# An attention-like kernel on one core: loads of batches 1 to 4 issued first on GpSimd, weight casts moved into the schedule, PSUM banks reserved, the DMA queue modelled

## The chip, the cores and the metric

The kernel runs on one core of a Trainium2 chip. The metric is the device time of one execution in microseconds (us), median of several; the span that the profiler shows is some 2 us shorter. Fast executions of one kernel agree within about 0.5 % of each other on the first chip, so a version is compared with runs of the kernel before that were made on the same chip in the same rounds. A few executions fall in a slow state (over 1.5 % above the fastest of the same kernel, as 169.73 us beside 165.76 for before) and are left out of ratios.

## The reference, cut to what matters

Eight batches of 4224 rows of 192 channels. Each row is first mixed with the six rows before it (one softmax over 7 taps for each of 8 heads); then comes linear attention without a softmax, and an output product.

```python
# x: (8, 4224, 192), weight: (8, 7), w_q and w_k: (192, 64), w_out: (192, 192)
w   = softmax(weight)                                # per head, over the 7 taps
y   = sum_k w[h, k] * x_pad[:, s + k, h, :]          # causal, 6 zero rows in front
wq, wk = y @ w_q, y @ w_k
W   = (1 / 8) * wq @ wk.T                            # no softmax on it
out = relu(W @ y) @ w_out
```

Since nothing nonlinear stands between the two products, `W @ y` is computed as `wq @ (wk.T @ y)`, and `wk.T @ y = w_k.T @ (y.T @ y)`. The kernel's names follow: `Y` (the 7-tap mix, as banded matmuls from `xw`), `G` = y.T y, `GS`/`GT` (G copied to SBUF, and transposed parts of it), `M` = the small matrix from G and w_k, `Q` = y w_q, `Z` = relu(Q M), `O` = Z w_out.

## The kernel before

All instructions are put in order at build time by a list scheduler. It keeps a clock for each engine and, at every step, places the job whose inputs it believes ready first. What it believes of data from DMA is a table of constants. Each engine's stream is thus fixed, and in the traces an instruction that waits holds what stands behind it: in experiment 8 ScalarE stands 1.50 us for w_k, and the copies of Y that come after its casts begin only at 17.17 us.

```python
CLOCK = {   # when the schedule believes that things are there, us
    "x0": (6.0, 7.4, 7.9, 9.0, 10.2, 12.3, 14.2, 15.5), "band": 6.5, "wq": 7.0, "wk": 17.0,
    "wo": 20.0, "x": (20.6, 10.3), "store": 5.0, "now": 0.05, "hold": 1.5, "fill": 24.0,
    "issue": 3.2,
}
# ... batch 0 is loaded in eight pieces x0_0 to x0_7, every later batch in two halves
ident = pool(lambda e: e.memset(IDENT[:, :], 0.0))
ident = pool(lambda e: e.affine_select(IDENT[:, :], ...), [ident])
z_zr  = pool(lambda e: e.memset(ZR[:, :, 1, :], 0.0))
zero = {1: clear(1)}                  # two memsets on GpSimd
load(1, 0)                            # first half of batch 1: DMAs issued by GpSimd
# ... jobs are defined ...
cast("wk", WK[:, 0], twice(WST[:, 0, 0:DH]), [wl[1]])     # six casts of w_k on GpSimd
# ...
load(1, 1)                            # second half of batch 1
cast("wo", WO1[:, :], WST[:, 2, :], [wl[2]])              # four casts of w_out on GpSimd
# ...
for b in range(2, 1 + AHEAD):         # AHEAD = 2
    for part in range(2):
        prefetch(b, part)             # clear and load batch 2
# later batches: two batches ahead, after the job that duplicates Y of a half batch
if kind == "D" and job.name[1] > 0:
    prefetch(job.name[1] + AHEAD, job.name[2])
```

GpSimd thus does three things: it issues all loads of x, it casts the weights to bf16, and it makes the duplicates of Y (`COPY y<-y`). The stores are issued by SyncE.

## Time and profile before

| kernel before | |
|---|---|
| time, median of 3 runs | 166.16 us (165.76 to 169.73) |
| span of the profiled run, granted clock of TensorE | 164.8 us, 0.943 |
| TensorE busy | 144.3 us, 88 % |
| real matmul work (see below) | 131.9 us |
| start of the first matmul with data / of the last matmul | 6.6 / 157.1 us |

The page's own summary: TensorE busiest, and half of the chain that ended last is TensorE. "PE" is TensorE, DVE VectorE, ACT ScalarE, POOL GpSimd; the shares of the second line are of the span.

```profile
span 164.8 us, 5806 instructions
...
PE 144.3 (88%) x2518; PEld 108.4 (66%) x2547; DVE 114.7 (70%) x218; ACT 127.4 (77%) x224; POOL 68.5 (42%) x99
...
PE 50%; ACT 23%; DMA 8%; POOL 6%; issue 5%; DVE 3%; ACTq 0%; POOLq 0%
```

Busy time hides how much of it is useful: the page counts a `G` matmul as busy for 193 ns on average, and where nothing holds them they follow each other every 29 ns. So I use a second measure in this text, **work done**: the weight loads of the trace in program order, each matmul taken at the pitch at which its kind recurs where nothing holds it (a 512-column one 0.219 us, a 432-column one 0.184, a 384-column output 0.168, a `G` 0.029, a `Q` 0.0186); the rows of `warm` matmuls (the expectations say "warming"), whose results nothing reads, count nothing. The whole kernel is 131.9 us of work. "Lost" is the time on the clock less the work done by then.

The DMA view of 0 to 45 us, in 40 slices of 1.1 us, shows the hole that the change is aimed at: the rate falls to 148, 130, then 127 and 38, then 19 and 88 GB/s.

```profile
DMA  0059999999999999996999938999999999999999
GB/s 0 10 94 141 198 181 188 188 188 187 189 205 148 130 196 209 194 127 38 184 189 194 175 19 88 193 190 193 189 155 303 349 263 184 334 351 238 193 198 190
```

GpSimd's timeline says why (columns: start, us taken, engine, line, operation, out<-in, count, and in brackets the idle time before with what ended it). It waits 2.15 us for w_k and casts for 2.15 us before it issues batch 1's second half at 18.59, and comes to batch 2 at 23.82.

```profile
16.50 2.15 POOL L797 CAST wk<-wst 128x128 bf16<-128x128 f32 x6 [2.15 <-DMA wst<-in_moe_w_k_dram]
18.59 1.78 POOL L265 DMA_DIRECT2D xw<-in_x_dram  x2
...
23.82 4.78 POOL L265 DMA_DIRECT2D xw<-in_x_dram  x6 [0.30 <-POOL xw L442]
28.58 0.69 POOL L281 DMA_DIRECT2D xw<-in_x_dram  x1
```

The chain of waits of 36 to 56 us (start, us, what) shows where this load lateness reaches TensorE: the last piece of batch 2, issued at 28.58, lands at 42.20, and TensorE's timeline has it waiting for that for 1.19 us before 42.34. ("Issue" is time in which an engine waits for nothing that the profile shows.)

```profile
28.58 13.62 DMA xw<-in_x_dram
42.20 0.14 issue
```

```profile
16.10 0.45 PE L595 MATMUL ps<-yb,wq 32*64 32x288 bf16 x15 [0.69 <-issue]
...
42.34 0.32 PE L530 MATMUL ps<-xw,band 128*128 128x384 bf16 x1 [1.19 <-DMA xw<-in_x_dram]
44.79 0.36 PE L743 MATMUL ps<-wo,zt 128*128 128x192 bf16 x2 [1.17 <-ACT y L898]
```

Note for later what is *not* there: between 15 and 42 us no wait of TensorE is put down to a load of x in this timeline. (Sooner than 15 us batch 0's pieces are waited for, much of it under `warm` matmuls; the change leaves those loads alone.)

### The profile page before, as it was taken

The numbers are of one execution on the slowest core, as the hardware profiler recorded it, in microseconds if no ns is written. First come the engines' busy times: TensorE is split into PE (matmuls) and PEld (weight loads), VectorE is DVE, ScalarE is ACT, GpSimd is POOL, SyncE is SP. The second block draws the span as 40 slices with busy tenths as digits, with TensorE's granted clock in tenths as the row PEclk, the third lists the DMA queues.
The fourth block names the chain that finished last, engine by engine and source line by source line (L and its number), as shares of the span: only waits on it lengthen the run. The fifth ranks groups of instructions, "written<-read, shape, count | busy, mean of one in ns | idle before, by whom it ended". The sixth has DMA issues, their size and how long they took to land.

```text
span 164.8 us, 5806 instructions
## 1 busy us (share of the span) xinstructions
PE 144.3 (88%) x2518; PEld 108.4 (66%) x2547; DVE 114.7 (70%) x218; ACT 127.4 (77%) x224; POOL 68.5 (42%) x99
## 2 busy tenths in 40 slices
PE   5897879699499998999899998999999989999920
PEld 4886734477377777677577866777777767766710
DVE  6784849769467677789788876877967686585500
ACT  5552559686589898788888997979998968799940
POOL 7984989888871807063804562202011200000000
PEclk9999999999999999999999999999999999999996
DMA  3999999999999999999999999999985472678896
GB/s 48 190 188 167 166 162 112 190 275 285 193 191 285 260 225 290 337 231 296 243 330 265 309 223 344 296 282 204 358 309 187 191 279 107 219 296 338 311 397 237
DMA packets 48281, 40.44 MB, mean 245 GB/s; under 512 B 38144, under 2 KB 40320, under 8 KB 48256
## 3 DMA queue, kind: packets, MB, share of 16 engines
q0 software_dynamic: 36784, 13.63, 70.2%
q1 hardware_dynamic: 11472, 26.45, 44.2%
q8 instruction: 20, 0.33, 0.7%
q14 instruction: 5, 0.04, 0.1%
HBM read 27.73 MB, written 25.95 MB: 326 GB/s over the span
## 4 chain that ended last, share of the span: by engine, by line
PE 50%; ACT 23%; DMA 8%; POOL 6%; issue 5%; DVE 3%; ACTq 0%; POOLq 0%
PE ps L624 12%; ACT o_sb L898 8%; DMA xw<-in_x_dram 8%; PE ps L530 8%; PE ps L595 7%; PE ps L743 7%; ACT y L898 7%; PE ps L745 6%; PE ps L700 5%; ACT zt L901 4%; POOL xw L265 4%; PE ps L499 2%; DVE y L898 2%; ACT zr L901 1%; DVE shift L405 1%
## 5 line engine op out<-in xcount | busy, mean ns | idle before, releaser
L898 ACT CAST y<-ps 128x864 bf16<-128x864 f32 (+5 forms) x59 | 48.2, 832 | 6.2 <-PE ps L499 3.1
L898 ACT COPY o_sb<-ps 128x768 f32<-128x768 f32 (+1 forms) x54 | 41.1, 783 | 6.2 <-PE ps L745 5.5
L743 PE MATMUL ps<-wo,zt 128*128 128x192 bf16 x256 | 43.1, 251 | 3.1 <-ACT y L898 1.3
L902 DVE TENSOR_SCALAR zt<-ps 128x512 bf16<-128x512 f32 x52 | 34.4, 684 | 13.4 <-PE ps L700 9.1
L745 PE MATMUL ps<-wo,zt 128*128 128x384 bf16 x128 | 42.5, 332 | 0.0
L265 POOL DMA_DIRECT2D xw<-in_x_dram x51 | 40.7, 803 | 2.1 <-POOL xw L442 1.3
L898 POOL COPY y<-y 128x1152 bf16<-128x1152 bf16 x14 | 16.1, 1148 | 57.6 <-ACT y L898 41.0
L624 PEld LDWEIGHTS ps<-y 128*128 128x128 bf16 x864 | 33.2, 98 | 9.9 <-issue 1.4
L624 PE MATMUL ps<-y 128*128 128x64 bf16 x864 | 36.7, 193 | 0.6 <-DVE y L898 0.2
L743 PEld LDWEIGHTS ps<-wo,zt 128*128 128x128 bf16 x256 | 25.5, 115 | 12.7 <-ACT o_sb L898 1.4
L896 DVE STREAM_TRANSPOSE yb<-y 128x576 int32<-128x576 int32 x48 | 33.7, 748 | 0.2 <-ACT y L898 0.2
L530 PE MATMUL ps<-xw,band 128*128 128x432 bf16 (+1 forms) x112 | 29.3, 340 | 2.0 <-DMA xw<-in_x_dram 1.2
L901 ACT ACTIVATE zt<-ps 128x512 bf16<-128x512 f32 x44 | 26.2, 622 | 0.9 <-PE ps L700 0.8
L700 PE MATMUL ps<-qt,m_sb 128*128 128x512 bf16 x67 | 22.7, 390 | 2.9 <-ACT y L898 0.9
L898 ACT CAST qt<-ps 128x576 bf16<-128x576 f32 (+2 forms) x23 | 12.2, 565 | 12.4 <-PE ps L595 12.3
L898 DVE CAST qt<-ps 128x234 bf16<-128x234 f32 (+1 forms) x25 | 9.6, 423 | 12.3 <-PE ps L595 12.2
L898 DVE COPY o_sb<-ps 128x768 f32<-128x768 f32 (+1 forms) x18 | 14.8, 821 | 4.7 <-PE ps L745 3.4
L595 PE MATMUL ps<-yb,wq 32*64 32x288 bf16 x768 | 16.0, 287 | 1.9 <-issue 1.5
L898 DVE CAST y<-ps 128x864 bf16<-128x864 f32 (+3 forms) x13 | 11.6, 896 | 5.1 <-PE ps L530 3.5
L745 PEld LDWEIGHTS ps<-wo,zt 128*128 128x128 bf16 x128 | 14.5, 113 | 0.0
L530 PEld LDWEIGHTS ps<-xw,band 128*128 128x128 bf16 x112 | 9.8, 99 | 6.6 <-DVE yb L896 1.3
L595 PEld LDWEIGHTS ps<-yb,wq 32*64 32x64 bf16 x768 | 10.5, 103 | 4.5 <-issue 2.4
(74 smaller groups left out, 113.3 us busy)
## 6 DMA issues: line engine op xcount, KB each, us to landing
out_dram<-o_sb SPq DMA_DIRECT2D x31, 768.0 KB, 7.2
xw<-in_x_dram POOLq DMA_DIRECT2D x21, 384.0 KB, 15.3
xw<-in_x_dram POOLq DMA_DIRECT2D x7, 432.0 KB, 17.3
xw<-in_x_dram POOLq DMA_DIRECT2D x4, 240.0 KB, 5.1
out_dram<-o_sb SPq DMA_DIRECT2D x16, 48.0 KB, 5.7
out_dram<-o_sb SPq DMA_DIRECT2D x2, 384.0 KB, 3.5
xw<-in_x_dram POOLq DMA_DIRECT2D x8, 42.0 KB, 9.4
xw<-in_x_dram POOLq DMA_DIRECT2D x1, 288.0 KB, 5.4
```

The source lines that it names most:

```text
L265: return e.dma_start(XW[lo:hi, b % NX, half, c : c + n, :], bass.AP(x_t, at, [[D, hi - lo], [CW * D, n], [1, D]]),)
L499: last = e.matmul(o, band_[:, h, :], rhs, start=True, stop=True, skip_group_check=True)
L530: last = e.matmul(o.rearrange("p (c h d) -> p h c d", h=2, d=GRP), band_[:, h, :], rhs, start=True, stop=True, skip_group_check=True,)
L595: last = e.matmul(PS[64 * h : 64 * h + 64, bk + i, 0:288], WQ[r, j, :], rhs, start=j == 0, stop=j == 5, skip_group_check=True)
L624: last = e.matmul(PS[:, 7, 64 * k : 64 * k + 64], y[:, 64 * k : 64 * k + 128], y[:, 64 * k : 64 * k + 64], start=c + h + k == 0, stop=c == ...
L700: return e.matmul(PS[:, bk, :], m[:, parts[k] : parts[k] + 128], q, start=True, stop=True)
L743: e.matmul(o[:, 192 * h : 192 * h + 192], z[:, h, cols], WO1[:, :], start=h == 0, stop=False, **kw)
L745: last = e.matmul(o[:, 0:384], z[:, 2, cols], WO2[:, :], start=False, stop=True, **kw)
L896: return e.transpose(o, i)
L898: return e.copy(o, i) if eng == "act" else e.tensor_copy(o, i)
L901: return e.activation(o, i, AF.Relu)
L902: return e.tensor_scalar(o, i, 0.0, None, op0=ALU.max)
```

## The change

The intent: keep the load queue full. GpSimd issues the loads of batches 1 to 4 first, one after the other; the casts of w_k and w_out become jobs of the schedule, which gives them to ScalarE or VectorE; the zero rows of batches 1 and 2 are cleared by ScalarE; w_k and w_out are loaded a little earlier. The schedule gets a model of the DMA queue (a rate, a delay, loads and stores sharing it) in place of fixed times for x. The stream of `Q` jobs is asked first at each step, so that its four banks are reserved before another job takes them, and some cost constants are new.

```diff
 CLOCK = {
-    "x0": (6.0, 7.4, 7.9, 9.0, 10.2, 12.3, 14.2, 15.5), "band": 6.5, "wq": 7.0, "wk": 17.0,
-    "wo": 20.0, "x": (20.6, 10.3), "store": 5.0, ...
+    "x0": (6.0, 7.7, 8.2, 9.4, 10.6, 12.5, 13.5, 14.3), "band": 6.6, "wq": 7.1, "wk": 14.0,
+    "wo": 17.0, ...
+    "dma": (377e3, 13.8, 1.6, 0.8),
 }
...
-        wload(2 * s, 0, 128, src, 0, wd, wl[s + 1], [xg[0][3 + 2 * s]])
+        wload(2 * s, 0, 128, src, 0, wd, wl[s + 1], [xg[0][2 + 2 * s]])
...
-    zero = {1: clear(1)}
     load(1, 0)
+    load(1, 1)
+    ident = pool(lambda e: e.memset(IDENT[:, :], 0.0))
+    ...                                       # affine_select, z_zr
+    for b in range(2, NX):                    # NX = 5
+        load(b, 0)
+        load(b, 1)
...
-    cast("wk", WK[:, 0], twice(WST[:, 0, 0:DH]), [wl[1]])
-    ...
-    load(1, 1)
-    cast("wo", WO1[:, :], WST[:, 2, :], [wl[2]])
-    ...
+    casts = [
+        job_w("wk", 0, WK[:, 0], twice(WST[:, 0, 0:DH]), 128, 1),
+        ...
+    ]
...
     streams = {
+        "Q": [job_q(b, g) for b in range(B) for g in range(2)],      # was behind "Z"
+        "W": casts,
...
-    EASY = {"act": 1.0, "dve": 0.3, "pool": 2.0}
+    EASY = {"dve": 0.55, "pool": 1.3}
...
+    RATE, at0, DELAY, LAND = CLOCK["dma"]
+    def flow():                               # shares RATE between loads and stores
+        ...
-                if key[1] > 0:
+                if key[1] > 1:                # duplicates of batch 1 no longer on GpSimd
                     eng = "pool"
...
-            prefetch(job.name[1] + AHEAD, job.name[2])
+            prefetch(job.name[1] + NX - 1, job.name[2])
```

The diff moves far fewer lines than instructions: since the schedule decides by its clocks, the whole order changes. In the order as built TensorE does batch 1's Y and half of batch 2's before the first output matmul.

## The prediction

> **What bounds the kernel now.** From about 55 us on, TensorE: the chain of waits there is mostly matmuls, and Q products recur every 17.2 us per batch (71.9, 89.0, 106.8, 124.2, 140.6 us). Summing matmul columns at the pitch of the timeline (512 columns in 0.224 us, a Q group in 0.89) gives 132 us of real work, 16.6 per batch. It runs between 6.6 and 157.5 us; the last evacuation and store take the other 7.3 us of the 164.8 us span. So TensorE loses about 19 us, mostly early: by 55.5 us it has done 35 us of work, 13.6 lost since 6.6; later it loses 5.
>
> **Why the early stage loses.** The load queue starves because GpSimd issues late. While loads are queued the DMA rate is about 188 GB/s of bf16 written (376 read), but the 0 to 45 us window shows 130 at 14 us, 38 near 18.5, 19 and 88 near 26 to 28. The GpSimd timeline has the causes: memsets and the affine select (9.2 to 11.3), a 2.15 us wait for w_k and 2.15 us of casts (14.4 to 18.6) ahead of batch 1's second half, wo casts and clears up to 23.8 ahead of batch 2. That is some 3.6 us of idle queue. Batch 2's second half then meets the first stores and lands at 42.3, 13.6 us after its last issue, with TensorE waiting. [...] from 34 to 42 us loads and stores together read and write an estimated 375 GB/s.
>
> **What the change does.** GpSimd issues batches 1 to 4 nearly back to back (5.5 us each), from 9.2 to about 32 us, so the queue should not starve. A half batch takes 4.5 to 4.7 us at 376 GB/s: batch 1 lands near 19.5 and 24, batch 2 near 28.5 and 33. The ten casts (0.3 us each) and batch 1's copies go to ScalarE and VectorE: some 5 us more on two engines, between 14 and 33 us, where I estimate both nearly full. In the built order TensorE does batch 1's Y, most of its G, half its Q and half of batch 2's Y before the first output matmul (now at 27.2 us); stores start later. Work, tail order and the 6.6 us start are unchanged.
>
> **Sum.** At 33.5 us I expect 21 us of work done, against 18; the wait at 42 and gaps around it go, so 35 us is reached near 48.5 instead of 55.5. From these 7 us I give back 2 for waits on ScalarE and VectorE and for full overlap of loads and stores (52 MB at 375 GB/s is 139 us). Net 5 us.
>
> **Predicted:** 161 us, range 158 to 164.5; faster by over 2%: 0.76; within 2%: 0.21; slower: 0.03.
>
> **What would show it.** Right: DMA full from 3 to 45 us; no TensorE wait on x after 30 us; batch 2's second Q group 5 to 7 us earlier; 17.2 us per batch later; the same tail. Wrong: TensorE waiting for batch 2's x while output matmuls that could fill the gap stand behind it; ScalarE and VectorE saturated; output copies waiting for stores.
>
> **What would make it wrong.** Landings later than the schedule's model, met by an in-order TensorE[...].

7 us won less 2 given back is net 5, from about 166 us to 161. The 375 GB/s is the author's estimate; the trace of before has, from 34 to 42 us, 0.73 MB of loads (bf16 as written; the f32 read is twice that) and 1.53 MB of stores, together 374 GB/s. The 52 MB are x read and the result written, 25.95 MB each.

## The result, and the profile after

| | before | after |
|---|---|---|
| time, median | 166.16 us (165.76 to 169.73, 4 runs) | 163.89 us (163.59 to 164.41, 4 runs) |
| ratio of fast runs, 95 % interval | | 0.9874 (0.9837 to 0.9912) |
| span of the profiled run, granted clock | 164.8 us, 0.943 | 162.4 us, 0.977 |
| first output matmul | 27.2 us | 38.5 us |
| batch 2's second `Q` group starts | 54.6 us | 53.7 us |
| last matmul starts | 157.1 us | 155.4 us |

A ratio here and below is the mean time of one kernel's fast runs over that of the other's fast runs of the same rounds, so it is not quite the ratio of the medians. The change is worth 1.3 %, not the 3.1 % predicted: it is 2.3 us faster, within 2 %, and inside the upper end of the range. Run again on two other chips it gave 163.9 (0.982, interval 0.9774 to 0.9867) and 164.07 us (0.9877, interval 0.9837 to 0.9916).

The page after, the lines that answer to those above. TensorE now makes up 74 % of the chain. The clock row (tenths of full speed, 40 slices) has a dip between 16 and 24 us (0.5 for 3.41 us, from 18.5 on).

```profile
span 162.4 us, 5831 instructions
...
PE 146.9 (90%) x2547; PEld 109.3 (67%) x2547; DVE 118.5 (73%) x230; ACT 128.8 (79%) x228; POOL 61.9 (38%) x83
...
PEclk9999779999999999999999999999999999999995
...
PE 74%; ACT 8%; DMA 6%; POOL 4%; issue 3%; DVE 1%; ACTq 0%; POOLq 0%
```

The load queue does what was wanted of it. It is full from 3 to 45 us:

```profile
DMA  0059999999999999999999999999999999999999
GB/s 0 8 104 145 196 171 189 173 173 175 187 192 197 195 228 208 193 192 191 199 183 187 191 192 191 193 199 189 185 189 190 211 177 192 192 191 189 189 199 187
```

GpSimd issues batch 1's second half before 15 us, batch 2 from 15.67 and batch 3 from 22.10:

```profile
7.66 6.34 POOL L264 DMA_DIRECT2D xw<-in_x_dram  x8
...
15.67 4.79 POOL L264 DMA_DIRECT2D xw<-in_x_dram  x6
...
22.10 4.79 POOL L264 DMA_DIRECT2D xw<-in_x_dram  x6 [0.29 <-POOL xw L437]
```

Batch 2's last piece is there at 35.83 in place of 42.20 us (last of its 16 parts, from the DMA records), and the wait at 42 us is gone. TensorE's timeline has no wait for x after 18 us. And yet TensorE is not ahead:

```profile
16.75 0.51 PE L503 MATMUL ps<-xw,band 128*128 128x96 bf16 x8 [1.62 <-DMA xw<-in_x_dram]
...
18.07 1.29 PE L599 MATMUL ps<-yb,wq 32*64 32x288 bf16 x48
...
21.84 0.60 PE L956 MATMUL ps<-warm 128*128 128x128 bf16 x7
...
25.43 0.95 PE L599 MATMUL ps<-yb,wq 32*64 32x288 bf16 x48 [0.66 <-DVE y L945]
...
31.82 0.40 PE L599 MATMUL ps<-yb,wq 32*64 32x288 bf16 x9 [0.87 <-issue]
```

The measure of work done says where the 2.3 us come from. The rows are profiled runs; the runs of the last three rows are explained below. The measure is good to some 0.2 us.

| run | 5 us of work done at | 20 us | 25 us | 35 us | 130 us | span |
|---|---|---|---|---|---|---|
| before | 16.1 | 37.0 | 44.8 | 55.0 | 155.2 | 164.8 |
| before, another chip | 16.6 | 37.1 | 45.4 | 55.4 | 155.2 | 164.9 |
| after | 17.8 | 38.9 | 44.0 | 54.1 | 152.1 | 162.4 |
| after, second chip (no clock dip) | 15.7 | 37.9 | 43.4 | 53.5 | 151.5 | 161.5 |
| after, third chip | 15.7 | 38.5 | 43.7 | 53.7 | 151.7 | 161.3 |
| after, batches 1 and 2 not loaded, third chip | 16.1 | 38.4 | 43.5 | 53.6 | 151.6 | 161.6 |
| before, batches 1 and 2 not loaded | 15.8 | 35.5 | 42.1 | 53.0 | 152.2 | 161.8 |
| after, times of the schedule corrected, third chip | 16.5 | 37.1 | 42.8 | 53.0 | 151.0 | 160.1 |

At 20 us of work the kernel after is *later* than before, by 1 to 2 us. It gains about 3 us on the next 5 us of work, where the wait at 42 us was. At 35 us of work it leads by 0.9 us (by about 1.8 on the other chips), where the prediction had 6.5 to 7. The rest, another 2 us or so, comes between 35 and 130 us of work, of which the prediction said nothing.

Both parts show in the groups of the page (line, engine, operation, out<-in, shapes, count, then busy us and mean ns, then the idle time just before and what ended most of it). Before:

```profile
L700 PE MATMUL ps<-qt,m_sb 128*128 128x512 bf16 x67 | 22.7, 390 | 2.9 <-ACT y L898 0.9
...
L530 PE MATMUL ps<-xw,band 128*128 128x432 bf16 (+1 forms) x112 | 29.3, 340 | 2.0 <-DMA xw<-in_x_dram 1.2
```

and after:

```profile
L704 PE MATMUL ps<-qt,m_sb 128*128 128x512 bf16 x96 | 33.7, 380 | 0.3 <-DVE qt L945 0.3
...
L534 PE MATMUL ps<-xw,band 128*128 128x432 bf16 (+1 forms) x112 | 28.7, 336 | 0.0
```

The Y matmuls (L530, L534) wait 2.0 us less, 1.2 of it the wait at 42 us: that is the early part. The Z matmuls (L700, L704) wait 2.6 us less, and that is most of the late part. From 55 us on the waits view of before has 2.2 us in which they wait for ScalarE or VectorE (2.3 in its second profile); after has one wait there, 0.9 us before an output matmul. (0.5 us more of before's 2.9 may be missing matmuls: its trace has records of 67 of the 96.) That the Z matmuls no longer wait is the new order's doing; which of its parts (reserved banks, new cost constants, output jobs later) is not told apart by any run here.

### The profile page after: what moved, and what is told of

It is laid out like the page before. It is cut to its first block, busy times and chain, and to the rows that moved or that the text cites. A ratio compares the mean times of both kernels' runs of the same rounds, so it can differ in the third digit from the quotient of the medians.

```text
span 162.4 us, 5831 instructions
## 1 busy us (share of the span) xinstructions
PE 146.9 (90%) x2547; PEld 109.3 (67%) x2547; DVE 118.5 (73%) x230; ACT 128.8 (79%) x228; POOL 61.9 (38%) x83
## 3 DMA queue, kind: packets, MB, share of 16 engines
HBM read 27.73 MB, written 25.95 MB: 331 GB/s over the span
## 4 chain that ended last, share of the span: by engine, by line
PE 74%; ACT 8%; DMA 6%; POOL 4%; issue 3%; DVE 1%; ACTq 0%; POOLq 0%
PE ps L628 15%; PE ps L747 13%; PE ps L534 12%; PE ps L704 12%; PE ps L749 11%; PE ps L599 9%; DMA xw<-in_x_dram 6%; ACT o_sb L945 5%; POOL xw L264 4%; ACT zt L948 1%; ACT y L945 1%; PE ps L668 1%; ACT m_sb L950 1%; DVE y L945 1%; PE ps L707 1%
## 5 line engine op out<-in xcount | busy, mean ns | idle before, releaser
L945 ACT CAST y<-ps 128x864 bf16<-128x864 f32 (+5 forms) x58 | 46.5, 827 | 4.8 <-PE ps L503 4.5
L945 ACT COPY o_sb<-ps 128x768 f32<-128x768 f32 (+1 forms) x60 | 44.5, 773 | 5.4 <-PE ps L749 4.2
L949 DVE TENSOR_SCALAR zt<-ps 128x512 bf16<-128x512 f32 x60 | 40.0, 681 | 8.6 <-PE ps L704 8.4
L749 PE MATMUL ps<-wo,zt 128*128 128x384 bf16 x128 | 41.7, 326 | 0.0
L264 POOL DMA_DIRECT2D xw<-in_x_dram x51 | 40.7, 812 | 1.5 <-POOLq L1091 0.8
L945 POOL COPY y<-y 128x1152 bf16<-128x1152 bf16 x12 | 13.8, 1153 | 66.3 <-ACT y L945 52.6
L704 PE MATMUL ps<-qt,m_sb 128*128 128x512 bf16 x96 | 33.7, 380 | 0.3 <-DVE qt L945 0.3
L534 PE MATMUL ps<-xw,band 128*128 128x432 bf16 (+1 forms) x112 | 28.7, 336 | 0.0
L948 ACT ACTIVATE zt<-ps 128x512 bf16<-128x512 f32 x36 | 21.5, 622 | 0.8 <-PE ps L704 0.6
L945 DVE CAST qt<-ps 128x288 bf16<-128x288 f32 (+1 forms) x31 | 11.9, 425 | 13.2 <-PE ps L599 13.0
L945 ACT CAST qt<-ps 128x576 bf16<-128x576 f32 (+1 forms) x17 | 10.5, 625 | 11.9 <-PE ps L599 11.8
L599 PE MATMUL ps<-yb,wq 32*64 32x288 bf16 x768 | 16.1, 288 | 2.0 <-issue 1.3
L534 PEld LDWEIGHTS ps<-xw,band 128*128 128x128 bf16 x112 | 9.6, 97 | 5.1 <-issue 1.6
L704 PEld LDWEIGHTS ps<-qt,m_sb 128*128 128x128 bf16 x96 | 8.9, 97 | 5.5 <-ACT zt L948 0.8
```

Source lines behind the costliest of these rows:

```text
L264: return e.dma_start(XW[lo:hi, b % NX, half, c : c + n, :], bass.AP(x_t, at, [[D, hi - lo], [CW * D, n], [1, D]]),)
L534: last = e.matmul(o.rearrange("p (c h d) -> p h c d", h=2, d=GRP), band_[:, h, :], rhs, start=True, stop=True, skip_group_check=True,)
L599: last = e.matmul(PS[64 * h : 64 * h + 64, bk + i, 0:288], WQ[r, j, :], rhs, start=j == 0, stop=j == 5, skip_group_check=True)
L704: return e.matmul(PS[:, bk, :], m[:, parts[k] : parts[k] + 128], q, start=True, stop=True)
L749: last = e.matmul(o[:, 0:384], z[:, 2, cols], WO2[:, :], start=False, stop=True, **kw)
L945: return e.copy(o, i) if eng == "act" else e.tensor_copy(o, i)
```

## The experiments

Eighteen runs were made, on five more chips. The letters in the quoted expectations name these theories, as I held them at the time:

- **D**: data of batches 1 and 2 still come too late (the last of the 16 parts of a load lags: in the first profile of after half of those of batch 0's seventh piece are there by 12.62 us, the last at 16.70).
- **S**: the now full load queue holds up batch 0's last pieces (16.70 and 17.47 us in that profile, 13.50 and 15.90 in before).
- **W**: ScalarE and VectorE stand still in order for w_k, whose casts the schedule put ahead of copies of Y.
- **E**: the chain through the engines (copies out of PSUM, transposes, the small matrix M, order) limits TensorE until 40 us, not the loads.
- **F**: TensorE waits for its own instructions (blocks of them, see experiment 9).

These are guesses; what the runs show of each is said after "Measured".

Others are said in the quotations themselves. Diffs are against the kernel after unless said otherwise. "Before" in a result is the kernel before in the same rounds.

### 1. Hold back batch 1: is the full queue the trouble?

```diff
+    zero[1].append(xg[0][4])      # batch 1's loads wait for batch 0's fifth piece
     load(1, 0)
     load(1, 1)
```

> The changed kernel, with one more wait: GpSimd's first load of batch 1 waits until the fifth load of batch 0 has landed on all 16 shares of the DMA engines (10.6 to 11.8 us), so that batch 1's issue starts near 11 us instead of 9.16. Theory S (a full load queue lets one engine's share of each load fall behind, so the last shares of batch 0 land at 16.7 and 17.5 us although their medians are 12.6 and 13.8): the last two loads of batch 0 land by about 14 and 16 us, batch 1's first half still lands by 22.5 us though it is issued 2 us later, and the time stays within 0.5 us of the changed kernel or falls by up to 1 us. Rival Q (landing is set by bytes ahead in the queue; the late landing is chance or the weight loads): batch 0's last loads land at 16.5 to 17.5 us as before and batch 1's first half 2 us later than 22.5.

Measured: 167.13 us, ratio to before 1.0046 (0.9939 to 1.0153). Batch 0's last two pieces landed at 14.26 and 15.16 us and batch 1's first half at 20.51. S had said so, but the kernel after without the hold lands them at much the same times (14.41 and 15.39 on the second chip, 14.80 and 15.39 on the third). So a full queue alone does not explain the 16.70 and 17.47 of the first profile of after; what made the last of the 16 parts late there stays open. The time did not stay within 0.5 us, as S had it. The run lost its time elsewhere, in one wait on GpSimd:

```profile
43.35 0.77 PE L629 MATMUL ps<-y 128*128 128x64 bf16 x12 [4.26 <-POOL y L946]
```

GpSimd makes the duplicate of batch 2's Y only after the loads of batches 1 to 4 and what follows them in its stream; with the loads held back that copy ended at 43.3 us. This is a gate that the change itself built: in the kernel after the copy ends at 40.7, just in time. It comes back in experiment 9.

### 2. Correct the schedule's times: is the order built on wrong beliefs?

The schedule of after believes that w_k is there at 14.0 (the traces: 16.1 to 16.6) and batch 0's last piece at 14.3 (15.4 to 17.5). Three kernels differ only in such constants; no instruction is added or taken away.

```diff
-    "x0": (6.0, 7.7, 8.2, 9.4, 10.6, 12.5, 13.5, 14.3), ... "wk": 14.0, "wo": 17.0,
-    "dma": (377e3, 13.8, 1.6, 0.8),
+    "x0": (6.0, 8.1, 8.6, 9.7, 11.8, 13.7, 16.7, 17.5), ... "wk": 16.5, "wo": 18.8,
+    "dma": (377e3, 17.0, 1.6, 0.8),
```

All of it:

> The changed kernel with the schedule's landing times set to those measured in its own trace (batch 0: 6.0, 8.1, 8.6, 9.7, 11.8, 13.7, 16.7, 17.5; w_k 16.5, w_out 18.8; load queue 3.2 us later). Same loads, other TensorE order: the first Q group now stands before batch 0's last Y products, and output products come before batch 1's second half. Theory O (the loss is in-order TensorE meeting loads later than the model believed): 1.5 to 3 us faster than the changed kernel, about 161.5 us. Rival D (the data are late and the early work is bound by them and by the evacuations whatever the order): within 0.7 us of the changed kernel.

The first line alone:

> The changed kernel with only batch 0's and the weights' landing times in the schedule set to the measured ones; the load queue's model as in the change. If the cost of the order lies in the first Q group standing behind batch 0's last Y products, about as fast as the full refit (1.5 to 3 us below the changed kernel). If it lies in batches 1 and 2 being believed 3 us too early, within 0.7 us of the changed kernel.

The second line alone:

> The changed kernel with only the load queue's model 3.2 us later; batch 0's landing times as in the change. The opposite of the run above: 1.5 to 3 us below the changed kernel if the loss lies in batches 1 and 2 believed too early (output products then come earlier in TensorE's order); within 0.7 us of it if it lies in batch 0's order.

Measured: all of it 161.97 us, ratio 0.9728 (0.9664 to 0.9793), without the kernel after in its rounds (experiment 10 has them side by side). On another chip, beside 163.9 us for after in the same rounds: the first line alone 162.54 us, 0.9712 (0.9659 to 0.9764); the second alone 167.04 us, 1.0026 (0.997 to 1.0083). So order alone moves this kernel by about 2 us down and 3 us up, as much as the whole change. The corrected times help, but not because each belief is nearer the truth: the second line is nearer too, and alone it costs 3 us. With it batch 3's first half lands at 45.9 instead of 39.1 us; that this is the cause is not shown, for after 16 us no wait of TensorE in that trace is put down to a load. Nor do the traces bear out the place of the gain that the expectations name. The first line alone has 20 us of work done at 39.1 us (37.9 in after on that chip) and wins later, the second alone at 37.0 us and loses later. The first total is about what was forecast for it, a loss of 3 us was in neither forecast, and the reason for either is not shown.

### 3. In the kernel before, only issue batch 1's first half sooner

```diff
 # on the kernel before
+    zero = {1: [act(lambda e: e.memzero(XW[0:6, 1, 0, 0, :])),
+                act(lambda e: e.memzero(XW[:, 1, :, NCK - 1, :]))]}   # clears on ScalarE
...
-    zero = {1: clear(1)}
     load(1, 0)
+    ident = pool(...)          # ident and z_zr moved behind the load
```

> The kernel before, with one part of the change: GpSimd's memsets between batch 0's and batch 1's loads are moved behind batch 1's first half (clears on ScalarE), so its issue starts at 9.2 us instead of 11.3; casts, order and all else of before. Theory S: batch 0's last two loads now land late (after 15.5 and 16.8 us against 13.5 and 15.9), batch 1's first half lands no more than 1 us earlier than 20.7, and the time does not fall (165.5 to 167). Rival Q: batch 0 lands as in before, batch 1's first half 2 us earlier (18.7), time down by up to 1 us.

Measured: 168.72 us, ratio 1.0105 (1.0011 to 1.0198); 20 us of work at 38.4 us, 1.4 later than in before. The edit did not fill the hole, it moved it: batch 1's first half, issued 2.2 us sooner, landed at 20.85 us (20.70 in before), and w_k at 17.56 (16.44), so that GpSimd cast it later and issued batch 1's second half at 19.72 (18.59). Batch 2's last piece came at 43.50 (42.20). What a filled hole is worth, this run does not tell.

### 4. Make the casts nearly free

```diff
-            evacs=[(lambda bk: [(o, i)], (name, k), n, "cast")],
+            evacs=[(lambda bk: [(o[..., 0:2], i[..., 0:2])], (name, k), n, "cast")],
```

Two columns instead of 64 to 192; the weights are zeroed instead, so the result is wrong.

> Wrong results on purpose. The changed kernel with its ten weight casts cut to two columns per block (the weights are zero elsewhere), same order and same waits. Theory C (the casts on ScalarE and VectorE cost what I gave back and more): M of batch 0 is ready 1 us earlier and the kernel is 1 us or more faster. Rival S or O: within 0.5 us, since ScalarE has idle time around the casts. [...]

Measured: 165.26 us, ratio 0.9894 (0.9798 to 0.999), no better than after. The first `Q` of batch 0 starts sooner (16.65 us), but w_k also landed sooner in this run (15.41 us). From landing to `Q` it is 1.24 us, in after on the third chip 1.55, so shorter casts gave some 0.3 us there. 20 us of work is done only at 39.6: before 31.70 TensorE stands 2.46 us with nothing to wait for ("issue"), in place of 0.9 us in after. Because of that pause (experiment 9) the total says nothing of the casts.

### 5. Batches 1 and 2 filled in place instead of loaded

The first try at taking the loads away wrote a constant into the slots with two memsets on GpSimd (result wrong).

```diff
-    load(1, 0)
-    load(1, 1)
+    for b in (1, 2):
+        filled[b] = pool(lambda e, b=b: e.memset(XW[:, b, :, :, :].bitcast(F32), 0.3715...), zero[b])
```

> Wrong results on purpose. The changed kernel, instruction for instruction on TensorE, ScalarE and VectorE, but batches 1 and 2 are not loaded: GpSimd fills their slots with a constant, done by about 14 and 18 us, well ahead of the landings at 22.5, 26.9, 31.5 and 35.8 us. Theory D (late data of batches 1 and 2 hold up TensorE between 20 and 36 us): 20 us of work is reached at least 3 us earlier (before 36 us instead of 38.9) and the total falls by 2 us or more. Rival E (the chains through evacuations, transposes and bank reuse set the pace there): 20 us of work is reached less than 1.5 us earlier. The time of batch 0's own landing moves as well, since its loads have the queue to themselves, so I compare from the first Q group on.

Measured: 169.42 us, ratio 1.0121. The trial spoiled itself. While GpSimd's memset ran (9.1 to 15.3 us), VectorE's bf16 copies took some ten times their usual time: each ended only when a memset did. Its timeline in this run:

```profile
12.20 0.58 DVE L949 CAST y<-ps 128x480 bf16<-128x480 f32 x1
12.71 2.64 DVE L949 COPY y<-y 128x320 bf16<-128x320 bf16 x1
```

against that of after on the third chip:

```profile
11.63 0.66 DVE L945 CAST y<-ps 128x480 bf16<-128x480 f32 x1 [1.24 <-PE ps L503]
12.33 0.26 DVE L945 COPY y<-y 128x320 bf16<-128x320 bf16 x1
```

The cast out of PSUM keeps its time (0.58 and 0.66 us), the copy from SBUF to SBUF goes from 0.26 to 2.64 us. It ends at 15.36, 0.08 us after the second memset (12.30 to 15.28); another copy, from 9.35 to 12.28, ends 0.10 us after the first. Why they share this time no run here shows.

### 6. Batches 1 and 2 read batch 0's slot

A cleaner way: Y of batches 1 and 2 is computed from batch 0's data, and those two batches are not loaded at all. TensorE, ScalarE and VectorE keep their order; the result is wrong.

```diff
+    SLOT = {0: 0, 1: 0, 2: 0, 3: 3, 4: 4, 5: 1, 6: 2, 7: 0}
-                    rhs = XW[:, b % NX, half, a0:a1, GRP * h : GRP * h + GRP]
+                    rhs = XW[:, SLOT[b], half, a0:a1, GRP * h : GRP * h + GRP]
...
-    load(1, 0)
-    load(1, 1)
...
-    for b in range(2, NX):
+    for b in range(3, NX):
```

First run:

> Wrong results on purpose. The changed kernel with the same order on TensorE, ScalarE and VectorE, but batches 1 and 2 are not loaded: their Y products read batch 0's slot, so their data are there from 15.4 us on. This replaces the run with the constant, in which GpSimd's memsets slowed VectorE. Theory D (late data of batches 1 and 2 hold up TensorE between 20 and 36 us): 20 us of work is reached by 35.5 us (37.9 in the changed kernel). Rival E (chains through evacuations, casts and transposes set the pace): not before 36.8 us. The later stage has a quarter less load traffic and is not compared.

Measured: 165.26 us, ratio 0.9881 (0.9818 to 0.9943), but its profiled run was slow, so its trace is not used. The second run stood beside the unchanged kernel after:

> The changed kernel as the reference of the three others on one chip: 163.4 to 164.9 us.

> Wrong results on purpose: data of batches 1 and 2 there from about 16 us on, order as in the change; again because the first profile fell among slow runs and had a clock dip. Rival E: from 10 to 20 us of work TensorE loses 1 to 1.6 us beside the pauses for instructions, as much as in the changed kernel (1.2), and 20 us of work is not reached before 36.5 us. Theory D: before 35.5 us.

Measured: after 164.07 us (0.9877, interval 0.9837 to 0.9916); with the data there from 16 us on 163.54 us (0.985, interval 0.98 to 0.9899). The intervals overlap almost wholly. The two traces are each other's twins. TensorE's waits in the kernel after, third chip:

```profile
17.66 1.60 PE L599 MATMUL ps<-yb,wq 32*64 32x288 bf16 x48 [1.60 <-ACT y L945]
...
25.06 0.96 PE L599 MATMUL ps<-yb,wq 32*64 32x288 bf16 x48 [0.88 <-DVE y L945]
...
27.09 0.38 PE L704 MATMUL ps<-qt,m_sb 128*128 128x512 bf16 x1 [0.61 <-DVE qt L945]
...
31.46 0.41 PE L599 MATMUL ps<-yb,wq 32*64 32x288 bf16 x9 [0.85 <-issue]
...
37.78 0.43 PE L599 MATMUL ps<-yb,wq 32*64 32x288 bf16 x11 [0.44 <-issue]
```

and with batches 1 and 2 not loaded:

```profile
17.60 1.67 PE L598 MATMUL ps<-yb,wq 32*64 32x288 bf16 x48 [1.16 <-ACT y L944]
...
24.96 0.95 PE L598 MATMUL ps<-yb,wq 32*64 32x288 bf16 x48 [0.88 <-DVE y L944]
...
26.89 0.38 PE L703 MATMUL ps<-qt,m_sb 128*128 128x512 bf16 x1 [0.51 <-DVE qt L944]
...
31.36 0.33 PE L598 MATMUL ps<-yb,wq 32*64 32x288 bf16 x8 [0.86 <-issue]
...
37.67 0.44 PE L598 MATMUL ps<-yb,wq 32*64 32x288 bf16 x11 [0.50 <-issue]
```

This settles D for the kernel after: loads of batches 1 and 2, early or late or absent, do not set its time. What does, between 16 and 38 us, is in those lines. The waits add up to 4.4 us (1.60, 0.88, 0.61, 0.85, 0.44). Between 21.5 and 22.7 us TensorE has only `warm` matmuls to run, 1.2 us, while `G` is copied out, transposed and copied again. And this run's clock dip (0.5 for 3.41 us, from 17.8 on) made one `Q` and one `G` group take 3.8 us for 2.3 us of work. Together that is 7.1 of the 7.8 us lost there. None of it is a load of x.

### 7. In the kernel before, take the same two batches' loads away

If loads do not limit the kernel after, how much did they ever limit the kernel before? That is the size of the prediction's main term. The same edit, on the kernel before:

> Kernel before with the loads of batches 1 and 2 left out: their Y products read batch 0's slot, so their data lie there from about 16 us; the order on TensorE, ScalarE and VectorE is that of before (result wrong on purpose). Theory E (in the kernel before, late loads cost only the one wait for batch 2's second half at 42 us): 20 us of work at 36.5 to 37.6 us as in before (37.0, 37.1), 25 us of work at 42 to 43 us in place of 44.8 to 45.4, total 162.5 to 164.5 us. Rival L, the step of the prediction (a starved load queue makes TensorE lose about 7 us by 55 us): 20 us of work at 34 us or sooner, 35 us of work at 50 us or sooner, total under 161 us.

Measured: 163.82 us, ratio to before 0.9833 (0.9769 to 0.9897). Theory E is right on the total and on 25 us of work (42.1 us), and off by a microsecond on 20 us of work (35.5). L is wrong on all counts: 35 us of work is done at 53.0 us, not 50 or sooner. The wait for x at 42 us is gone; what comes there now is the wait for a copy of ScalarE, the one that before had at 44.79:

```profile
42.12 0.36 PE L746 MATMUL ps<-wo,zt 128*128 128x192 bf16 x2 [1.14 <-ACT y L901]
```

So all that early data for batches 1 and 2 could give, in the order of the kernel before, is 1.7 % (1.0 to 2.3), about 3 us of span (164.9 to 161.8). And this is too much rather than too little: the run also frees GpSimd and the queue of a quarter of all loads. About 1.4 us of the 3 are no load at all. In before TensorE stands for 0.69 and 0.77 us in front of 16.10 and 21.92 us (0.80 and 0.55 in its second profile), pauses that experiment 9 explains; here both are missing, and that is the microsecond and a half by which 20 us of work came sooner:

```profile
15.15 1.04 PE L598 MATMUL ps<-yb,wq 32*64 32x288 bf16 x48 [0.18 <-DVE y L901]
```

### 8. Load w_k at once: is it the wait for w_k?

In the kernel after ScalarE and VectorE come to the casts of w_k before it has landed, and copies of Y stand behind them. ScalarE's timeline, third chip:

```profile
14.05 0.58 ACT L945 CAST y<-ps 128x504 bf16<-128x504 f32 x1 [1.65 <-PE ps L503]
16.13 1.01 ACT L945 CAST wk<-wst 128x128 bf16<-128x128 f32 x4 [1.50 <-DMA wst<-in_moe_w_k_dram]
17.17 1.20 ACT L945 CAST y<-ps 128x336 bf16<-128x336 f32 x3
```

In before those casts were on GpSimd and the first `Q` group ran at 14.6 us; here it starts at 17.7. The edit lets w_k's load wait for nothing; the order of all instructions stays:

```diff
-        wload(2 * s, 0, 128, src, 0, wd, wl[s + 1], [xg[0][2 + 2 * s]])
+        wload(2 * s, 0, 128, src, 0, wd, wl[s + 1], [xg[0][4]] if s else [])
```

Run with the kernel before again, and with a version whose schedule was also told the measured times:

> The kernel before itself, for a second profile of it: ratio 1.00 within 0.5 %. Its first profile had a granted clock of 0.949 all through, all profiles of the changed kernel and its variants 1.0 with at most one dip of 3.4 us. If the clock belongs to the kernel, 0.95 again; if to the chip or the execution, 1.0 here, and then TensorE's loss after 55 us falls from 5 us to about 3.

> The changed kernel, same order on every engine, with one wait taken away: the loads of w_k no longer wait for batch 0's third load, so w_k lands by about 8 to 10 us instead of 16.5. Theory W (ScalarE and VectorE run in order; the casts stand before batch 0's last Y evacuations and hold them until w_k lands at 16.5, and with them the first Q group): ScalarE and VectorE no longer idle from 15.3 to 16.6 us, the first Q group starts 1 us or more earlier (17 instead of 18.1), and the total falls by 1 us or more, to 162.9 or less against 163.9. Rival: the casts' wait is hidden behind batch 0's own late landing; within 0.4 us of the changed kernel.

> Candidate that should beat both kernels: the changed kernel with w_k loaded at once and the schedule's landing times set to those measured (batch 0 at 6.1 to 15.5, w_k 9, w_out 17.8, load queue 1.8 us later). 160.5 to 162.5 us, 0.96 to 0.97 of the kernel before. If orders differ by luck more than by these waits, it may as well be 163 to 165.

Measured: before against itself 1.0056 (1.0008 to 1.0104), which is how far two sets of runs of one kernel can lie apart. Its clock was 1.0 this time (mean over the span 0.992, against 0.943), so the 0.95 does not belong to the kernel, but 35 to 130 us of work took 99.8 us against 100.2: the fall of 2 us that I expected of it did not come. Early w_k gave 165.15 us, 0.9959 (0.992 to 0.9997); with the schedule told of it 163.59 us, 0.9861 (0.9822 to 0.99), not the 160.5 to 162.5 hoped for. In the early w_k run w_k landed at 9.4 instead of 16 us and the wait for it was gone: the first `Q` started at 16.80. The gain did not last. At 31 us TensorE stood for 2.45 us in place of 0.86, released by nothing. On the third chip, beside the kernel after:

> w_k loaded early, order as in the change, now beside the changed kernel on one chip. Theory W alone: 1 us faster than it. Theory W with F ([...]where TensorE is ahead it stands still in the second batch's first Q group until the block is there, 2.45 us instead of 0.86): no faster than the changed kernel, within 0.5 us or up to 1.3 us slower, with the first Q group 1 us or more earlier and a pause of more than 2 us at the 39th product of that later Q group.

Measured: 164.8 us, 0.9901 (0.9846 to 0.9957), beside 164.07 for after: no gain, and the same pause:

```profile
32.70 0.40 PE L599 MATMUL ps<-yb,wq 32*64 32x288 bf16 x9 [2.45 <-issue]
```

But the first `Q` started at 17.57 us on this chip, only 0.1 us sooner than in after; the forecast of 1 us or more was met on the one chip and missed on the other. So of W it is shown that the engines' wait for w_k is real and goes away. That this wait sets the start of the first `Q` is not shown (the casts still stand ahead of copies of Y and take 1.0 us of ScalarE), and it explains nothing of the total. The run of after on the second chip belongs here too; it is the one without a clock dip, beside the runs of experiments 2 (one constant alone) and 5:

> The changed kernel itself once more, as the measure of its neighbours on this chip: 163.5 to 165.5 us, 0.985 to 0.99 of the kernel before. Its own landings again, to see how much the last share of a load lags from chip to chip: theory S expects the last two loads of batch 0 between 14 and 17.5 us.

Measured: 163.9 us, 0.982 (0.9774 to 0.9867). With the dip (first chip 163.89, third 164.07 us) or without, the time is the same; the half-speed stretch is not what the prediction missed.

### 9. Is the pause a wait for instructions?

In the runs with this order the pause comes after the 39th or 40th matmul of the same `Q` group. The trace's instruction queue moves blocks of 16 KB, 20 in all for TensorE's 5121 instructions, so 256 in each, in about 0.95 us a block. In the early w_k run of the third chip TensorE had begun 959 instructions when such a fetch began at 30.33 and still 959 when it ended at 31.31; it went on at 32.70. To test the link, the row of `warm` matmuls that comes before all data is cut from 20 to 4, which takes 32 instructions (a weight load and a matmul each) out of the stream ahead of everything else:

```diff
 # on the early w_k version
-    warm(20, [])
+    warm(4, [])
```

> Kernel after with w_k loaded early (as in the early w_k run) and the second row of warming matmuls cut from 20 to 4, so that TensorE's instruction stream is 32 instructions shorter from there on; all else in the same order. In the early w_k runs TensorE stood 2.45 us after the 39th matmul of a Q group near 30 us, with nothing that it waited for. Theory F (it waits for its next block of instructions): the pause comes 32 instructions, 16 matmuls, later in the order: that Q group of 48 runs in one piece and a pause of 0.5 to 2.5 us comes about 7 matmuls after it. Rival Q (it belongs to the Q group itself): it stays after the 39th matmul. Total 163.5 to 166 us either way.

Measured: 163.87 us, 0.9861 (0.976 to 0.9962). That `Q` group ran in one piece:

```profile
28.87 0.95 PE L599 MATMUL ps<-yb,wq 32*64 32x288 bf16 x48
...
36.91 0.35 PE L749 MATMUL ps<-wo,zt 128*128 128x384 bf16 x1 [0.87 <-issue]
...
40.75 0.52 PE L628 MATMUL ps<-y 128*128 128x64 bf16 x12 [1.48 <-POOL y L945]
```

So the pause does not belong to the `Q` group: 32 instructions fewer, far upstream, and it is gone. Theory F's own forecast was met only in half: the place 16 matmuls later (30.41 us) passed without a pause; the fetch of that block had begun at 27.99. But the next pause, 0.87 us before 36.91, is at the next block. Counting TensorE's instructions in the 19 profiled runs that were fast settles it. Of 38 pauses of 0.2 us or more that the profile calls "issue", 37 come where TensorE has begun 193 instructions plus a multiple of 256 (449, 705, 961, 1217, 1473, 2497, 2753 or 3009, less the few records that a trace misses), in `Q`, `O` and `G` groups alike, and each ends 1.28 to 1.60 us after the end of an instruction fetch. (The other, 0.22 us in experiment 3, stands beside `Z` matmuls, of which that trace has lost records.) The kernel before has two of them before 25 us, at 449 and 705 (0.69 and 0.77 us). They are waits for the next block of instructions. From the *start* of its fetch it is 2.2 to 2.5 us until TensorE goes on, in all 37; a pause is what is left of that. The four of 2.45 or 2.46 us are those where the fetch began 0.01 to 0.09 us after TensorE had come to the end of its block; in the others it had begun 0.95 us or more before. What makes a fetch begin early or late, no run here shows.

And now the gate of experiment 1 shuts. With early w_k and without the pause, 20 us of work was done at 35.7 us, 2.8 sooner than in after. At 40.75 TensorE waited 1.48 us for GpSimd's duplicate of batch 2's Y, which stands behind the loads:

```profile
38.81 0.73 POOL L280 DMA_DIRECT2D xw<-in_x_dram  x1
39.49 1.20 POOL L945 COPY y<-y 128x1152 bf16<-128x1152 bf16 x1
```

GpSimd's copy starts at 39.5 in this run and in the unchanged one (39.52 on the third chip): its stream is full of load issues and nothing upstream moves it. Of the 2.8 us, 0.3 are left at 25 us of work (43.4 against 43.7).

### 10. The better version

The corrected schedule of experiment 2, timed again beside the kernel after:

> The schedule refitted to measured landings, beside the changed kernel on one chip. Theory O: 1.2 to 2.5 us faster than the changed kernel, 161.5 to 162.8 us, and 2 % or more faster than the kernel before. If the first comparison owed its gain to the chip, within 0.7 us of the changed kernel.

Measured: 162.07 us (161.62 to 162.29), ratio to before 0.9759 (0.9718 to 0.98); after in the same rounds 164.07 us. It beats both kernels, by 2.4 % and, as the quotient of the two ratios, 1.2 %. Its first `Q` starts at 15.9 us, since w_k's casts are now placed after copies of Y, and its first output matmul comes at 28.2 us, near the 27.2 of before.

## Why the prediction was wrong, point by point

- **"From about 55 us on, TensorE"**: right. 35 to 130 us of work take 98.0 us after and 100.2 before.
- **"The load queue starves because GpSimd issues late"**, and the change fills it: right, by the GB/s rows. The landings that I gave came some 3 us later than predicted (batch 1 at 22.5 and 26.9, batch 2 at 31.5 and 35.8 us, against 19.5, 24, 28.5 and 33), but experiment 6 shows that this did not matter.
- **"TensorE loses about 19 us, mostly early: by 55.5 us it has done 35 us of work, 13.6 lost since 6.6"**: the number was right. Its reading was the mistake. Of these 13.6 us 4.5 are lost by 16.1 us, on batch 0, whose loads the change does not touch. The text put the rest under "Why the early stage loses. The load queue starves", with waits of TensorE for x to show for 1.2 us of it.
- **"At 33.5 us I expect 21 us of work done, against 18; the wait at 42 and gaps around it go, so 35 us is reached near 48.5 instead of 55.5"**: this is the step that failed. At 33.5 us the kernel after had done 15.5 us of work (before: 16.6), and reached 35 us at 54.1 (before: 55.0). The term "starved loads", put at 7 us, measures about 3 us at most: that is what experiment 7 gains when batches 1 and 2 need no load at all (2.0 to 2.4 us of it at 35 us of work), and some 1.4 us of that are waits for instructions. The other waits that before's timeline lists between 16 and 55 us, 4.8 us, are for copies of ScalarE and VectorE and for instructions; early data left those for ScalarE as they were (0.33, 0.98 and 1.14 us in experiment 7). Half of the step was right, and it is the half with a wait behind it: 20 to 25 us of work took 7.8 us before and 5.1 after, once batch 2's second half came in time.
- **"I give back 2 for waits on ScalarE and VectorE"**: the mechanism was named, but it was taken off a gain that was not there. In the kernel after (third chip) a copy of Y behind w_k's casts ends the 1.6 us wait of the first `Q`, and later copies end waits of 0.9 and 0.6 us. The engines were not "nearly full" (an estimate given without its numbers): from 14 to 33 us ScalarE is busy for 65 % and VectorE for 73 % of the time in the first profile of after. TensorE waited for single copies late in their order.
- **"Batch 2's second Q group 5 to 7 us earlier"**: 0.9 us (54.6 to 53.7). **"No TensorE wait on x after 30 us"**: right. **"17.2 us per batch later", "the same tail"**: the second `Q` groups of batches 2 to 7 recur every 16.7 us; the tail is 0.7 us shorter (start of the last matmul to end, 7.7 and 7.0 us). The later stage is faster than predicted by 2.2 us. The prediction had no reason for that, so it is luck that hides part of the miss; without it the time would have been near that of before.
- **"What would make it wrong. Landings later than the schedule's model, met by an in-order TensorE"**: landings were later, and in-order engines met them, but not where I looked: none of batches 1 and 2 held TensorE, and w_k's (96 KB) held two copying engines. Experiments 8 and 9 show that taking that wait away gains nothing in the total, as other waits follow, first the one for instructions, then the one for GpSimd.

In short: the early loads removed one wait for x, of 1.2 us (1.7 in the second profile of before); the new order lost 1 to 2 us ahead of it and won some 2 us long after it. I had costed the resource (3.6 us of idle queue and its consequences) and not the wait.

Open: what makes a fetch of instructions come late in some orders; which part of the new order gave the 2 us after 35 us of work; and why the corrected schedule is faster in its later part, which only its total and its work table show.

## What to carry to other kernels

Before you credit a starved queue with an engine's lost time, list that engine's waits in the stage and add up those that name the queue; here that was 1.2 us of some 9 lost between 16 and 55 us. The cheapest test of such a term is to take the data need away (let later batches read data that are already there) and run the *old* kernel: it shows what early data are worth in that order, before any of the change is built. It does not bound a version that also changes the order (the corrected schedule gained 2.4 %, this test 1.7 %). And where a scheduler places everything, compare its constants with the trace first, since here that moved the time by 2 us with no change to what is computed.
